# A sparse-attention block: one two-column addition for a coming tile's threshold and the present tile's sum

## The chip, the cores and the metric

The kernel runs on one core of a Trainium2 chip. What is measured is the device time of one execution in microseconds (us). The core has five engines that each work through their own queue in order: PE (TensorE, matrix products and transposes), DVE (VectorE), ACT (ScalarE), POOL (GpSimd) and SP (SyncE, which here only issues transfers). "PEld" is the loading of PE's weights, which runs beside PE.

## What is computed

The reference is an attention that keeps only scores near the largest of their row, then two feed-forward blocks, the second with a Fourier transform:

```python
scores = scale * np.matmul(q, k.transpose(0, 1, 3, 2))
thresh = np.max(scores, axis=-1, keepdims=True) - tau
scores = np.where(scores >= thresh, scores, -1000000000.0)
scores = scores - np.max(scores, axis=-1, keepdims=True)
attn = np.exp(scores)
attn = attn / (np.sum(attn, axis=-1, keepdims=True) + 1e-09)
return np.matmul(attn, v).astype(np.float32)
...
k = np.maximum(xk @ w_k, 0.0)
v = k * k @ w_v
r = 1.0 / (1.0 + np.exp(-(xr @ w_r)))
return (r * v).astype(np.float32)
...
X = np.fft.fft(np.fft.fft(x, axis=1), axis=2)
u = x + np.real(X)
```

with q, k and v of 4 batches, 8 heads, 576 rows and 64 columns, d_model 512, d_ff 1024, and a last feed-forward pair of 512 by 2048 weights after a normalization of u. Only the attention is touched by the change.

## The kernel before, in words

The heads go in 16 pairs (4 batches by 4 pairs). A pair has nine score tiles of 128 query rows by 576 keys, so there are 144 tiles, called steps n = 0 to 143. The fifth tile of a pair, "em", holds the 64 last rows of both heads.

For each tile, PE makes the scores into a PSUM tile "s" (lines 227 and 241). DVE takes the negated row maximum from it (line 267). A threshold, maximum minus tau, is made from that by one small instruction on DVE (line 274), or for one tile of nine on ACT (line 272, chosen by the bit mask `TH`). ACT writes exp(score - maximum) into an SBUF tile "e" (line 278). DVE multiplies e by the mask "score at least threshold" and accumulates the row sum at the same time (line 282, which also shows as a short DVE_READ_ACCUMULATOR). Then DVE adds 1e-9 to the sum (line 633) and takes the reciprocal (line 637), and POOL, or ACT for some tiles, multiplies e by it (lines 289, 290 and 643). Two steps later PE transposes e (lines 329, 337, 349 and 352), ACT copies the result to SBUF "pt" and "ptr", and PE multiplies it with v ("av", line 388). All three small columns of a tile lie in one SBUF tile, "small", in nine groups of three.

Tiles 0 to 35 (batch 0) use plain float32 matmuls, and while they run PE has nothing but attention; DVE also splits the weights w_k and w_r into two parts meanwhile (lines 69 to 71, "wbits"), with ACT and POOL behind it (lines 75 and 79). In this stretch three score tiles are in flight, and the maximum is taken two steps ahead (`LX` is 2); from about step 34 on it is one step ahead and two score tiles are in flight. From the second batch on, the first feed-forward block of the batch before ("kps", "rps", "vps", lines 408 to 410 and 530 to 532) runs between the attention steps on PE, fed by "xtmp" and "xl" (lines 437 to 441), and w_v is split. Each later head pair loads "rawqk" into a single buffer, which DVE's line 196 frees. After the last step the transform and the last feed-forward block follow.

The order of all instructions is set by a scheduler at build time: the program emits the steps in a loop, each part with a priority offset from the table `P`, and the scheduler plays them through its own model and lays down a fixed order for each engine. The table is the same in both kernels. On an engine, an instruction that waits holds back all that stand behind it.

The functions that matter are `emit_max`, `emit_th`, `emit_exp`, `emit_select` and `emit_norm`, and `do_front`, which calls them for each step.

Of the kernel before, what the change touches and what calls it, by code (L numbers as in the profile page):

```python
# [10 lines left out]
F32 = mybir.dt.float32  # L11
F32R = mybir.dt.float32r
I32 = mybir.dt.int32
ALU = mybir.AluOpType
# [15 lines left out]
def tile_kernel(ctx: ExitStack, tc: tile.TileContext, a):  # L30
# [11 lines left out]
    small = const.tile([128, 46], F32, name="small")  # L42
    mus, cons, stats = small[:, 0:16], small[:, 16:19], small[:, 19:46]
# [103 lines left out]
    heads, vts, ptu, ptr, et, em, sps, stat, xT = ({} for _ in range(9))  # L147
# [116 lines left out]
    def emit_max(n):  # L264
        st = stats[:, 3 * (n % 9):3 * (n % 9) + 3]
        stat[n] = st
        dve.tensor_reduce(st[:, 0:1], sps[n][:, :, 0:HS], axis=AX.XY, op=ALU.max, negate=True)  # L267

    def emit_th(n):
        st = stat[n]  # L270
        if P['TH'] >> (n % 9) & 1:
            act.activation(st[:, 1:2], st[:, 0:1], AF.Identity, scale=-1.0, bias=cons[:, 1:2])
        else:
            dve.tensor_scalar(st[:, 1:2], st[:, 0:1], -1.0, cons[:, 1:2], op0=ALU.mult, op1=ALU.add)

    def emit_exp(n):
        st = stat[n]
        act.activation(two(eview(n)), sps[n][:, :, 0:HS], AF.Exp, bias=st[:, 0:1])  # L278

    def emit_select(n):  # L280
        st, e = stat[n], two(eview(n))
        dve.scalar_tensor_tensor(  # L282
            e, sps[n][:, :, 0:HS], st[:, 1:2], e, op0=ALU.is_ge, op1=ALU.mult, accum_out=st[:, 2:3]
        )

    def emit_norm(n):
        st, e = stat[n], eview(n)
        if n in em:
            pool.tensor_scalar(em[n][:, S:640], e[:, 512:S], st[:, 2:3], 1.0, op0=ALU.mult, op1=ALU.mult)
        pool.tensor_scalar(e, e, st[:, 2:3], 1.0, op0=ALU.mult, op1=ALU.mult)  # L290

    def emit_front(n):

        cur, nxt = 0 <= n < NSTEP, 0 <= n + 1 < NSTEP
        if cur:
            emit_select(n)
        if nxt:
            emit_max(n + 1)
        if cur:
            dve.tensor_scalar(stat[n][:, 2:3], stat[n][:, 2:3], 1e-9, None, op0=ALU.add)  # L300
        if nxt:
            emit_th(n + 1)
        if cur:
            dve.reciprocal(stat[n][:, 3:4], stat[n][:, 2:3])
            emit_norm(n)
# [263 lines left out]
    act.dma_start(cons[:, 2:3], a["tau"].to_broadcast([128, 1]))  # L569
    load_head(0, 0)  # L570
    load_head(0, 1, act, act)
    dve.memset(stats[:, 26:27], 0.0)
    act.activation(stats[:, 26:27], stats[:, 26:27], AF.Exp)

    tau = cons[:, 2:3]
    dve.tensor_scalar(cons[:, 0:1], tau, 0.0, 0.125, op0=ALU.is_ge, op1=ALU.mult)
    dve.tensor_scalar(cons[:, 1:2], tau, -1.0, 0.0, op0=ALU.mult, op1=ALU.min)
# [24 lines left out]
    for n in range(P['LX']):  # L602
        emit_max(n)
        emit_th(n)
        emit_exp(n)
# [10 lines left out]
    def do_front(n, pi, s):  # L616
# [3 lines left out]
        k = 1  # L620
        if s != 4 and P['SM' if pi >= NPAIR else 'SM0'] >> ((s - (s > 4)) // 2) & 1:

            k = 0 if s in (0, 2, 5, 7) else 2
        g = stats.rearrange("p (s c) -> p s c", c=3)[:, s + 1 - k:s + 1]
# [3 lines left out]
        with hp('pM'):  # L628
            for m in nxt:
                emit_max(m)  # L630
        with hp('pF'):
            if cur and k:
                dve.tensor_scalar(g[:, :, 2], g[:, :, 2], 1e-9, None, op0=ALU.add)
            for m in nxt:
                emit_th(m)
            if cur and k:
                dve.reciprocal(g[:, :, 2], g[:, :, 2])  # L637
        with hp('pN'):
            for m in range(n + 1 - k, n + 1):
                if cur:  # L640
# [723 lines left out]
```

## Time and profile before

| | us |
|---|---|
| median of 3 runs (1053.62 to 1055.33) | 1053.88 |
| the profiled execution, its own time | 1055.04 |
| its span, first to last instruction | 1053.0 |
| PE busy in the span | 1003.0 (95%) |
| DVE busy | 717.3 (68%) |
| ACT busy | 536.3 (51%) |
| POOL busy | 395.4 (38%) |

The shares are averages over stages with different limits: attention of batch 0 until about 118 us, attention with the first feed-forward block until about 510 us, and the transform with the last feed-forward block after that. In a row of the profile "idle before" is the time in which the engine stood still just ahead of these instructions, and after the arrow stands what ended it. A duration in the timeline runs from an instruction's start to its end; the next one on the same engine may start before that end, since an engine overlaps instructions that don't wait for each other. "PEclk" is the share of TensorE's full clock that was granted: 1.00 is 2.4 GHz.

### The profile page before, as it was taken

What the parts mean: (1) busy time and instruction counts of PE and PEld (TensorE: products, weight loads), DVE (VectorE), ACT (ScalarE), POOL (GpSimd) and SP (SyncE); (2) the same over time, 40 slices, a digit from 0 to 9 for tenths busy, and PEclk for the clock granted to TensorE, in tenths of its full rate; (3) what the DMA queues carried; (4) which work ended last, traced back from release to release, by engine and by line L of the source; (5) the groups of instructions that cost most, each with busy time, mean ns of one, the idle gap of its engine ahead of it and who ended that gap; (6) DMA issues with size and microseconds to landing.
All of it is one profiled execution on the core that took longest, in us unless ns stands there. A gap on an engine that the chain in (4) does not pass through costs nothing.

```text
span 1053.0 us, 18827 instructions
## 1 busy us (share of the span) xinstructions
PE 1003.0 (95%) x6807; PEld 884.1 (84%) x6807; DVE 717.3 (68%) x1880; ACT 536.3 (51%) x1211; POOL 395.4 (38%) x495
## 2 busy tenths in 40 slices
PE   6887779999999999999999989999999999999998
PEld 4565659988889888999889879898998888889997
DVE  6799988667776685865356889457537449236776
ACT  4688777675866766857265745243313113113332
POOL 1445868465584564844233100000014125112231
PEclk9899989999999999999999989999999999999999
DMA  6442332121211212100613666536325335223221
GB/s 228 146 133 80 118 108 60 48 67 43 72 60 48 73 31 88 51 24 14 198 55 110 202 204 200 159 127 207 119 92 180 130 119 175 96 101 120 101 100 61
DMA packets 45636, 114.52 MB, mean 109 GB/s; under 512 B 6319, under 2 KB 6740, under 8 KB 45544
## 3 DMA queue, kind: packets, MB, share of 16 engines
q1 hardware_dynamic: 27920, 74.47, 22.2%
q10 hardware_dynamic: 12344, 22.13, 6.8%
q0 software_dynamic: 5280, 16.72, 4.4%
q8 instruction: 54, 0.88, 0.4%
q14 instruction: 38, 0.31, 0.1%
HBM read 84.98 MB, written 28.32 MB: 108 GB/s over the span
## 4 chain that ended last, share of the span: by engine, by line
PE 74%; DVE 10%; DMA 6%; ACT 3%; issue 3%; POOL 2%; SPq 0%; ACTq 0%; DVEq 0%; POOLq 0%
PE c1ps L1090 7%; PE c1ps L1089 6%; PE c1ps L1088 6%; PE s L227 5%; PE av L388 5%; PE c2ps L1112 5%; PE c2ps L1110 5%; PE c2ps L1111 5%; PE p L1045 4%; PE t L329 4%; PE kps L408 2%; PE kps L409 2%; PE kps L410 2%; DMA rawqk<-in_qk 2%; PE vps L530 2%
## 5 line engine op out<-in xcount | busy, mean ns | idle before, releaser
L267 DVE TENSOR_REDUCE small<-s 128x1 f32<-128x576 f32 x144 | 106.9, 752 | 48.1 <-PE s L227 37.3
L1159 POOL DMA_DIRECT2D ud<-u x54 | 29.5, 546 | 264.2 <-DVE u L1158 206.3
L290 POOL TENSOR_SCALAR e<-e,small 128x576 f32<-128x576 f32 x112 | 90.1, 811 | 87.9 <-DVE small L637 73.5
L282 DVE SCALAR_TENSOR_TENSOR e<-s,small,e 128x576 f32<-128x576 f32 x128 | 102.7, 812 | 25.6 <-ACT e L278 22.4
L278 ACT ACTIVATE e<-s,small 128x576 f32<-128x576 f32 x128 | 93.9, 745 | 31.1 <-DVE small L267 27.9
L1100 ACT ACTIVATE hh<-c1ps 128x256 fp32r<-128x256 f32 (+1 forms) x84 | 37.1, 443 | 137.2 <-PE c1ps L1090 111.6
L1101 DVE SCALAR_TENSOR_TENSOR hh<-c1ps,hh 128x256 fp32r<-128x256 f32 (+1 forms) x84 | 41.6, 496 | 89.2 <-ACT hh L1100 89.2
L329 PE MATMUL t<-ident,e 128*128 128x128 f32 x512 | 82.5, 278 | 12.9 <-ACT pt L332 6.5
L332 ACT ACTIVATE pt<-t 128x512 f32<-128x512 f32 x128 | 75.2, 599 | 22.3 <-PE t L329 20.6
L329 PEld LDWEIGHTS t<-ident,e 128*128 128x128 f32 x512 | 61.2, 142 | 24.3 <-issue 6.9
L488 POOL TENSOR_TENSOR k<-relu,k 128x288 fp32r<-128x288 f32 x64 | 54.3, 851 | 68.1 <-ACT k L486 63.9
L408 PE MATMUL kps<-xh,wk 128*128 128x288 f32 x256 | 78.1, 306 | 1.7 <-DVE tg L537 0.9
L530 PE MATMUL vps<-k,wv 128*128 128x288 f32 x256 | 77.5, 304 | 0.4 <-ACT tg L518 0.4
L531 PE MATMUL vps<-k,wv 128*128 128x288 f32 x256 | 77.3, 303 | 0.0
L532 PE MATMUL vps<-k,wv 128*128 128x288 f32 x256 | 76.7, 301 | 0.0
L410 PE MATMUL kps<-xh,wk 128*128 128x288 f32 x256 | 76.2, 298 | 0.0
L409 PE MATMUL kps<-xl,wk 128*128 128x288 f32 x256 | 76.2, 298 | 0.0
L1090 PE MATMUL c1ps<-ut,cB 128*128 128x256 f32 (+1 forms) x256 | 76.0, 297 | 0.0
L1089 PE MATMUL c1ps<-ut,cB 128*128 128x256 f32 (+1 forms) x256 | 75.8, 296 | 0.0
L1088 PE MATMUL c1ps<-ut,cB 128*128 128x256 f32 (+1 forms) x256 | 75.7, 296 | 0.0
L1088 PE MATMUL c1ps<-ut,cA 128*128 128x256 f32 (+1 forms) x224 | 71.0, 317 | 1.4 <-ACT ut L1008 1.4
L1089 PE MATMUL c1ps<-ut,cA 128*128 128x256 f32 (+1 forms) x224 | 70.7, 316 | 0.0
(270 smaller groups left out, 3116.4 us busy)
## 6 DMA issues: line engine op xcount, KB each, us to landing
u<-ud SPq DMA_DIRECT2D x36, 512.0 KB
wraw<-in_w_ch ACTq DMA_DIRECT2D x64, 256.0 KB
rawqk<-in_qk SPq DMA_DIRECT2D x24, 608.0 KB
ud<-u POOLq DMA_DIRECT2D x54, 256.0 KB, 2.5
v<-in_v SPq DMA_DIRECT2D x16, 320.0 KB
un<-ud SPq DMA_DIRECT2D x18, 256.0 KB
out<-u SPq DMA_DIRECT2D x18, 256.0 KB
wraw<-in_w_k SPq DMA_DIRECT2D x8, 512.0 KB
```

The costliest lines, as they stand in the source:

```text
L267: dve.tensor_reduce(st[:, 0:1], sps[n][:, :, 0:HS], axis=AX.XY, op=ALU.max, negate=True)
L278: act.activation(two(eview(n)), sps[n][:, :, 0:HS], AF.Exp, bias=st[:, 0:1])
L282: dve.scalar_tensor_tensor(e, sps[n][:, :, 0:HS], st[:, 1:2], e, op0=ALU.is_ge, op1=ALU.mult, accum_out=st[:, 2:3])
L290: pool.tensor_scalar(e, e, st[:, 2:3], 1.0, op0=ALU.mult, op1=ALU.mult)
L329: pe.transpose(t[:, k, :], e[:, o + 128 * k:o + 128 * (k + 1)], ident)
L408: pe.matmul(ps, wh, x[0][k], start=(k == 0), stop=False)
L409: pe.matmul(ps, wh, x[1][k], start=False, stop=False)
L410: pe.matmul(ps, wl, x[0][k], start=False, stop=(k == nk - 1))
L530: pe.matmul(ps, wv[0][:, c:c + 128], k2[0][:, k, :], start=(k == 0), stop=False)
L1088: pe.matmul(ps, wh, ut[0][:, k, :], start=(k == 0), stop=False)
L1089: pe.matmul(ps, wh, ut[1][:, k, :], start=False, stop=False)
L1090: pe.matmul(ps, wl, ut[0][:, k, :], start=False, stop=(k == 3))
```

## The change

The sign of the scores is turned: the factor applied to q is -0.125 instead of 0.125. The row maximum becomes a row minimum (without negation), which is at once the bias of exp, whose scale is now -1. The threshold becomes minimum plus max(tau, 0), and the mask "score at most threshold". With that, the threshold of a coming tile and the sum of the present tile both come from adding a constant to a column: the minimum of the coming tile and the sum of the present one are written side by side into a block of four columns, and one addition of two columns with the constants (max(tau, 0), 1e-9) makes the threshold and the sum plus 1e-9, again side by side. The separate threshold instruction on DVE (line 274) or ACT (line 272) and the separate addition (line 633) are gone; the reciprocal stays. At the very start two tiles get a one-column addition, and one memset of a column is added.

```diff
-    small = const.tile([128, 46], F32, name="small")
-    mus, cons, stats = small[:, 0:16], small[:, 16:19], small[:, 19:46]
+    small = const.tile([128, 56], F32, name="small")
+    mus, cons, stats = small[:, 0:16], small[:, 16:20], small[:, 20:56]
...
-    def emit_max(n):
-        st = stats[:, 3 * (n % 9):3 * (n % 9) + 3]
-        stat[n] = st
-        dve.tensor_reduce(st[:, 0:1], sps[n][:, :, 0:HS], axis=AX.XY, op=ALU.max, negate=True)
-
-    def emit_th(n):
-        st = stat[n]
-        if P['TH'] >> (n % 9) & 1:
-            act.activation(st[:, 1:2], st[:, 0:1], AF.Identity, scale=-1.0, bias=cons[:, 1:2])
-        else:
-            dve.tensor_scalar(st[:, 1:2], st[:, 0:1], -1.0, cons[:, 1:2], op0=ALU.mult, op1=ALU.add)
+    def block(n):
+        return stats[:, 4 * (n % 9):4 * (n % 9) + 4]
+
+    def emit_min(n, at_step):
+        low[n] = block(at_step)
+        dve.tensor_reduce(low[n][:, 0:1], sps[n][:, :, 0:HS], axis=AX.XY, op=ALU.min)
+
+    def emit_add(n, ahead, cur):
+        c0, c1 = 0 if ahead else 1, 2 if cur else 1
+        g = block(n)
+        dve.tensor_tensor(g[:, 2 + c0:2 + c1], g[:, c0:c1], cons[:, 1 + c0:1 + c1], op=ALU.add)
...
-        act.activation(two(eview(n)), sps[n][:, :, 0:HS], AF.Exp, bias=st[:, 0:1])
+        act.activation(two(eview(n)), sps[n][:, :, 0:HS], AF.Exp, scale=-1.0, bias=low[n][:, 0:1])
...
-            e, sps[n][:, :, 0:HS], st[:, 1:2], e, op0=ALU.is_ge, op1=ALU.mult, accum_out=st[:, 2:3]
+            e, sps[n][:, :, 0:HS], low[n][:, 2:3], e, op0=ALU.is_le, op1=ALU.mult, accum_out=block(n)[:, 1:2]
...
             for m in nxt:
-                emit_max(m)
+                emit_min(m, n)
         with hp('pF'):
-            if cur and k:
-                dve.tensor_scalar(g[:, :, 2], g[:, :, 2], 1e-9, None, op0=ALU.add)
-            for m in nxt:
-                emit_th(m)
-            if cur and k:
-                dve.reciprocal(g[:, :, 2], g[:, :, 2])
+            if cur or nxt:
+                emit_add(n, len(nxt), cur)
+            if cur:
+                r = block(n)[:, 3:4]
+                dve.reciprocal(r, r)
```

The scheduler lays the order anew. Line numbers differ between the two kernels: the reduction is line 267 before and 269 after, the mask 282 and 281, the reciprocal 637 and 616, a transpose 329 and 313, and the new addition is line 274. First DVE's queue at the fourth weight piece of the first stretch ("wbits" is the weight, "small" the columns). Before:

```order
L267 TENSOR_REDUCE small<-s 128x1
L274 TENSOR_SCALAR small<-small 128x1
L267 TENSOR_REDUCE small<-s 128x1
L282 SCALAR_TENSOR_TENSOR e,small<-s,small,e 128x576
L69 TENSOR_SCALAR wbits<-wraw 128x512
L633 TENSOR_SCALAR small<-small 128x1
L70 SCALAR_TENSOR_TENSOR wbits<-wraw,wbits 128x512
L637 RECIPROCAL small<-small 128x1
L282 SCALAR_TENSOR_TENSOR e_368,small<-s,small,e_368 128x576
```

The same place after:

```order
L269 TENSOR_REDUCE small<-s 128x1
L71 SCALAR_TENSOR_TENSOR wbits<-wraw,wbits 128x512
L274 TENSOR_TENSOR small<-small 128x2
L616 RECIPROCAL small<-small 128x1
L281 SCALAR_TENSOR_TENSOR e,small<-s,small,e 128x576
L69 TENSOR_SCALAR wbits<-wraw 128x512
L379 COPY xt<-xt 128x1
L70 SCALAR_TENSOR_TENSOR wbits<-wraw,wbits 128x512
```

Two small instructions have become one, and it stands behind the reduction of a later tile; the reciprocal stands straight behind the addition, whose result it reads. Next PE's queue at the start of the program ("s" scores, "t" transposes). Before:

```order
L227 MATMUL s<-k,q 128x288 x8
L329 MATMUL t<-ident,e 128x128 x4
L241 MATMUL s<-k,q 128x288 x3
L241 MATMUL s<-k,q 128x224
L241 MATMUL s<-k,q 128x64
L227 MATMUL s<-k,q 128x288 x4
```

After:

```order
L227 MATMUL s<-k,q 128x288 x8
L241 MATMUL s<-k,q 128x288 x3
L241 MATMUL s<-k,q 128x224
L241 MATMUL s<-k,q 128x64
L227 MATMUL s<-k,q 128x288 x2
L313 MATMUL t<-ident,e 128x128 x4
```

The first four transposes have moved behind the scores of two more tiles. Last DVE's queue in the middle of the attention with the feed-forward block. Before:

```order
L267 TENSOR_REDUCE small<-s 128x1 x2
L274 TENSOR_SCALAR small<-small 128x1
L282 SCALAR_TENSOR_TENSOR e,small<-s,small,e 128x576 x2
L633 TENSOR_SCALAR small<-small 128x1 x2
L637 RECIPROCAL small<-small 128x1 x2
L537 SCALAR_TENSOR_TENSOR tg<-tg,vps 128x288
```

After:

```order
L269 TENSOR_REDUCE small<-s 128x1 x2
L274 TENSOR_TENSOR small<-small 128x2
L616 RECIPROCAL small<-small 128x1
L281 SCALAR_TENSOR_TENSOR em,small<-s,small,em 128x576
L274 TENSOR_TENSOR small<-small 128x2
L616 RECIPROCAL small<-small 128x1
```

Before, two tiles went through side by side, mask and mask, addition and addition; after, each tile's addition and reciprocal follow one another, and the next tile's mask comes behind them.

## Rows read from the trace of the kernel before

**Rows 1.** Share of busy tenths in 40 slices of the span.

```profile
PE   6887779999999999999999989999999999999998
...
DVE  6799988667776685865356889457537449236776
```

**Rows 2.** Busy time by stretch: start:end, length, each engine's busy time (count), PEclk.

```profile
12.00:40.00 28.00, 21.39 (x97) 14.27 (x96) 23.02 (x71) 16.46 (x31) 12.39 (x14) 0.88 0.59 194
40.00:80.00 40.00, 35.84 (x212) 25.95 (x211) 38.50 (x110) 32.43 (x67) 17.61 (x19) 1.00 0.41 123
80.00:110.00 30.00, 24.20 (x152) 16.66 (x151) 27.96 (x81) 23.14 (x46) 16.83 (x19) 1.00 0.34 100
110.00:150.00 40.00, 31.61 (x221) 26.41 (x219) 36.21 (x84) 27.79 (x62) 32.71 (x35) 0.96 0.34 105
150.00:510.00 360.00, 354.58 (x2712) 318.57 (x2713) 251.46 (x691) 247.46 (x564) 204.14 (x259) 1.00 0.17 52
```

**Rows 3.** DVE's groups from 12 to 150 us: busy, mean ns, idle before.

```profile
L267 DVE TENSOR_REDUCE small<-s 128x1 f32<-128x576 f32 x46 | 34.2, 747 | 1.5 <-PE s L227 1.3
L282 DVE SCALAR_TENSOR_TENSOR e<-s,small,e 128x576 f32<-128x576 f32 x39 | 31.5, 809 | 1.7 <-ACT e L278 1.3 <-ACT small L272 0.2
...
L274 DVE TENSOR_SCALAR small<-small 128x1 f32<-128x1 f32 x39 | 8.0, 206 | 0.2
...
L633 DVE TENSOR_SCALAR small<-small 128x1 f32<-128x1 f32 x45 | 6.4, 143 | 0.1
```

**Rows 4.** DVE's timeline at 17 us: start, duration; the next starts before the end.

```profile
17.17 0.21 DVE L274 TENSOR_SCALAR small<-small 128x1 f32<-128x1 f32 x1
17.29 0.14 DVE L633 TENSOR_SCALAR small<-small 128x1 f32<-128x1 f32 x1
17.35 0.68 DVE L71 SCALAR_TENSOR_TENSOR wbits<-wraw,wbits 128x512 int32<-128x512 int32 x1
```

**Rows 5.** DVE's timeline at 49 us: the reciprocal reads the addition ahead of it.

```profile
49.21 0.15 DVE L633 TENSOR_SCALAR small<-small 128x1 f32<-128x1 f32 x1
49.39 0.16 DVE L637 RECIPROCAL small<-small 128x1 f32<-128x1 f32 x1
```

**Rows 6.** DVE's timeline at 581 us, an addition of two columns in a later stage.

```profile
580.83 0.16 DVE L990 TENSOR_TENSOR lnst<-lnst 128x2 f32<-128x2 f32 x1
580.90 0.45 DVE L810 TENSOR_TENSOR H<-f,H 128x288 fp32r<-128x288 f32 x1
```

**Rows 7.** The chain that ended last, 10 to 150 us: shares by line, one piece.

```profile
by line: issue 9.6%; DVE e L282 8.2%; DVE small L267 8.1%; DMA wraw<-in_w_v 8.0%; PE s L227 7.9%; PE avs L388 6.9%; DMA rawqk<-in_qk 6.4%; PE t L329 3.9%; DVE wbits L71 3.7%; DVE wbits L69 3.5%; ACT e L278 3.4%; DVE wbits L70 3.3%; PE s L24
...
81.23 4.95 DMA rawqk<-in_qk
```

**Rows 8.** PE's timeline, 28 to 37 us.

```profile
30.00 1.11 PE L349 MATMUL tm<-ident,em 128*128 128x128 f32 x4 [3.27 <-POOL em L290]
...
33.92 3.53 PE L388 MATMUL avs<-pt,v 128*64 128x288 f32 x16
```

**Rows 9.** PE's timeline, 80 to 83 us: the same sixteen matmuls.

```profile
80.98 2.11 PE L388 MATMUL avs<-pt,v 128*64 128x288 f32 x16
```

**Rows 10.** Groups from 150 to 510 us: DVE's reduction, PE's transposes, POOL's multiplication.

```profile
L267 DVE TENSOR_REDUCE small<-s 128x1 f32<-128x576 f32 x98 | 72.8, 754 | 46.3 <-PE s L227 35.7 <-PE s L241 10.0
...
L329 PE MATMUL t<-ident,e 128*128 128x128 f32 x352 | 57.2, 274 | 0.2 <-ACT pt L356 0.2
...
L290 POOL TENSOR_SCALAR e<-e,small 128x576 f32<-128x576 f32 x88 | 69.6, 799 | 75.4 <-DVE small L637 61.1 <-DVE small L633 14.2
```

**Rows 11.** PE's timeline at 282 us: the spacing of feed-forward matmuls.

```profile
282.16 0.30 PE L409 MATMUL kps<-xl,wk 128*128 128x288 f32 x1
...
283.09 0.29 PE L410 MATMUL kps<-xh,wk 128*128 128x288 f32 x1
```

**Rows 12.** SP's queue around 100 us: issues of transfers.

```profile
98.55 0.33 SPq L56 DMA_DIRECT2D wraw<-in_w_v  x1
103.78 0.33 SPq L163 DMA_DIRECT2D rawqk<-in_qk  x1
```

More of the change, by code (lines that the diff above doesn't have):

```diff
@@ L146, in tile_kernel @@
     NSTEP = NPI * 9
-    heads, vts, ptu, ptr, et, em, sps, stat, xT = ({} for _ in range(9))
+    heads, vts, ptu, ptr, et, em, sps, low, xT = ({} for _ in range(9))
     def plain(pi):
@@ L276, in emit_exp @@
+    def emit_min(n, at_step):
[5 more added lines that the diff above has]
+        dve.tensor_tensor(g[:, 2 + c0:2 + c1], g[:, c0:c1], cons[:, 1 + c0:1 + c1], op=ALU.add)
     def emit_exp(n):
-        st = stat[n]
-        act.activation(two(eview(n)), sps[n][:, :, 0:HS], AF.Exp, bias=st[:, 0:1])
+        act.activation(two(eview(n)), sps[n][:, :, 0:HS], AF.Exp, scale=-1.0, bias=low[n][:, 0:1])
@@ L280, in emit_select @@
     def emit_select(n):
-        st, e = stat[n], two(eview(n))
+        e = two(eview(n))
         dve.scalar_tensor_tensor(
-            e, sps[n][:, :, 0:HS], st[:, 1:2], e, op0=ALU.is_ge, op1=ALU.mult, accum_out=st[:, 2:3]
+            e, sps[n][:, :, 0:HS], low[n][:, 2:3], e, op0=ALU.is_le, op1=ALU.mult, accum_out=block(n)[:, 1:2]
         )
     def emit_norm(n):
-        st, e = stat[n], eview(n)
+        r, e = block(n)[:, 3:4], eview(n)
         if n in em:
-            pool.tensor_scalar(em[n][:, S:640], e[:, 512:S], st[:, 2:3], 1.0, op0=ALU.mult, op1=ALU.mult)
@@ L290, in emit_norm @@
[L290 to L305, printed above, removed]
+            pool.tensor_scalar(em[n][:, S:640], e[:, 512:S], r, 1.0, op0=ALU.mult, op1=ALU.mult)
@@ L307, in unit @@
+        pool.tensor_scalar(e, e, r, 1.0, op0=ALU.mult, op1=ALU.mult)
     def unit(pi, half):
@@ L566, in ffn_stream @@
         yield from xt_out()
-    act.dma_start(cons[:, 2:3], a["tau"].to_broadcast([128, 1]))
+    act.dma_start(cons[:, 3:4], a["tau"].to_broadcast([128, 1]))
     load_head(0, 0)
     load_head(0, 1, act, act)
[L572 to L577, printed above, removed]
+    dve.memset(stats[:, 35:36], 0.0)
+    act.activation(stats[:, 35:36], stats[:, 35:36], AF.Exp)
+    dve.memset(cons[:, 2:3], 1e-9)
+    tau = cons[:, 3:4]
+    dve.tensor_scalar(cons[:, 0:1], tau, 0.0, -0.125, op0=ALU.is_ge, op1=ALU.mult)
+    dve.tensor_scalar(cons[:, 1:2], tau, 1.0, 0.0, op0=ALU.mult, op1=ALU.max)
     conv_k(0, 0)
@@ L602, in tile_kernel @@
     for n in range(P['LX']):
-        emit_max(n)
-        emit_th(n)
+        emit_min(n, n - P['LX'])
+        emit_add(n - P['LX'], True, False)
         emit_exp(n)
@@ L619, in do_front @@
         state['m'] = max(state['m'], n + ahead(n) + 1)
[L620 to L624, printed above, removed]
         with hp('pF'):
@@ L629, in do_front @@
             for m in nxt:
-                emit_max(m)
+                emit_min(m, n)
         with hp('pF'):
-            if cur and k:
-                dve.tensor_scalar(g[:, :, 2], g[:, :, 2], 1e-9, None, op0=ALU.add)
-            for m in nxt:
-                emit_th(m)
-            if cur and k:
-                dve.reciprocal(g[:, :, 2], g[:, :, 2])
-        with hp('pN'):
-            for m in range(n + 1 - k, n + 1):
-                if cur:
-                    if P['NA' if pi >= NPAIR else 'NA0'] >> (m % 9) & 1:
-                        e = eview(m)
-                        act.activation(e, e, AF.Copy, scale=stat[m][:, 2:3])
-                    else:
-                        emit_norm(m)
+            if cur or nxt:
[3 more added lines that the diff above has]
+                dve.reciprocal(r, r)
+        with hp('pN'):
+            if cur:
+                if P['NA' if pi >= NPAIR else 'NA0'] >> (n % 9) & 1:
+                    e = eview(n)
+                    act.activation(e, e, AF.Copy, scale=r)
+                else:
+                    emit_norm(n)
     def do_av(n, pi, s):
```

## The prediction, made before the changed kernel was run

> **What bounds the kernel now.** I read the busy shares by slice first. PE stands at nine tenths or more from the seventh slice on (a slice is 26.3 us) with two exceptions, and only the first six slices, up to about 158 us, lie below; there DVE has 9, 9 and 9 in the third to fifth [rows 1]. The table of stretches gives the sizes: from 12 to 150 us PE is busy 21.39 + 35.84 + 24.20 + 31.61 = 113.0 of 138 us, DVE 23.02 + 38.50 + 27.96 + 36.21 = 125.7, which is 91% [rows 2]. From 150 to 510 us PE is busy 354.6 of 360 us, so that 5.4 us is all that any other engine could give back there [rows 2]. After 510 us no instruction of the change runs. So the change is judged by the stretch from 12 to 150 us, in which PE idles 25 us.
>
> The chain of waits warns against taking DVE's 91% as the whole truth. In its shares for 10 to 150 us the named DVE lines (mask 8.2%, reduction 8.1%, weight split 3.7, 3.5 and 3.3%) with "issue" 9.6% make 36%; the rest are transfers of w_v and rawqk, PE and ACT, such as a rawqk transfer of 4.95 us that began at 81.23 [rows 7]. "Issue" pieces I count to DVE, since they lie between DVE's pieces. DVE's time therefore counts on the path with a weight between 0.36 and 0.91.
>
> **What the change takes away and adds.** *On DVE, per tile.* The threshold instruction lasts 206 ns, the addition of 1e-9 143 ns [rows 3]. But what they hold DVE for is less: the threshold starts at 17.17, the next instruction at 17.29, and the one behind the addition at 17.35, so the slots are 0.12 and 0.06 us [rows 4]. The new addition of two columns has a near relative in a later stage: 0.16 us long, the next instruction 0.07 us after its start [rows 6]. From 12 to 150 us 39 thresholds and 45 additions go, and about 46 new additions come, one for each reduction [rows 3]. Slots: 39 x 0.12 + 45 x 0.06 - 46 x 0.07 = 4.68 + 2.70 - 3.22 = 4.2 us less on DVE.
>
> *The hold.* An instruction that reads the result of the one straight ahead of it waits for its end: the reciprocal at 49.39 stands 0.18 us behind the addition at 49.21, not 0.07 [rows 5]. So a held place costs 0.11 us. In the laid-down order of the first 46 tiles 10 of the small instructions wait for the one straight ahead before, and 20 after (12 reciprocals, 8 additions). The 10 more cost 1.1 us. Net 4.2 - 1.1 = 3.1 us.
>
> Bounds of the new instruction: if none of the new ones were held longer than now, 4.2 us are gained. If every new addition held its follower (46 x 0.18 instead of 46 x 0.07), it would be 4.68 + 2.70 - 8.28 = -0.9 us, that is 0.9 us lost. I take 3.1 us, because the order says how many are held, and the 0.07 us row is the same operation on the same number of columns.
>
> *On the path.* 3.1 us x 0.36 = 1.1 us to 3.1 x 0.91 = 2.8 us. I take 2.8, since DVE's queue is what stands full from 40 to 110 us (66.5 of 70 us busy [rows 2]).
>
> *On ACT.* One tile in nine had its threshold made by ACT; the mask waited 0.2 us for that in this stretch [rows 3]. The wait goes: 0.2 us. Sum: 2.8 + 0.2 = 3.0 us.
>
> *At nothing.* The turned sign: reduction, exp, mask and the factor on q are the same instructions on as many elements with other constants. The memset of one column lies in the wait for the first inputs. From 150 to 510 us DVE loses about as much by slots as it gains by holds (99 tiles less, 151 held places against 82 by the order), and PE's 354.6 of 360 us covers the rest; without that cover up to 2 us would show.
>
> *Moved queues.* On SP's queue the third rawqk transfer (issued at 103.78, after a w_v piece at 98.55 [rows 12]) now stands behind one more w_v piece, and the fifth behind all eight. A w_v piece waits there until DVE has split the one before it, so a rawqk behind it starts some 4 us later. It is loaded a head pair ahead, and nine steps take 9 x 360 / 98 = 33 us in the long stretch [rows 2, 10], so I cost it at nothing; if that cover failed it would be 4 us once or twice. On POOL's queue the multiplication of the first "em" tile moves one 0.75 us multiplication ahead. PE's first four transposes move behind two tiles' scores; nothing on PE uses them before the first product with v.
>
> *The added wait.* The present tile's sum now goes through an instruction that also needs the coming tile's minimum, hence its scores on PE. Behind it wait the reciprocal, POOL's multiplication, and two steps later PE's transposes. From 150 to 510 us the reduction waits for scores 46.3 us in all, 0.47 us on each of 98 tiles, while transposes waited 0.2 us in all [rows 10]. What covers it is PE's own order: between the scores of a tile and the transposes of the one before it there stand at least 18 other PE instructions, before and after the change alike, typically some 50. At 0.133 us each (the first and the eighth of a series start at 282.16 and 283.09, 0.93 / 7 [rows 11]) 18 give 2.4 us. The way through is reduction 0.75, addition and reciprocal 0.2 each, POOL 0.75 to 0.8, about 2.0 us with no second tile ahead on POOL. It fits, barely at the worst five places. So no cost, but this is where a loss would come from.
>
> **A rule against my slots.** Rows 4 show the next independent instruction starting well before the end of a small one, rows 5 that a wait costs 0.11 us. The Trainium skill, VectorE: DVE Perf Modes, section "The DRAIN you can't avoid", says that the next operation does not start before the pipeline has emptied and that a semaphore after each of eight copies cost nothing extra; by it full durations count and holds are free. The same section allows that an operation that is not held starts earlier. The trace disagrees with the first half where nothing waits (0.12 us against 206 ns). What full durations would make of it, from rows: 39 x 0.206 + 45 x 0.143 - 46 x 0.157 = 8.03 + 6.44 - 7.22 = 7.2 us, x 0.91 = 6.6 us. I hold that as the first rival.
>
> **The sum.** Against the profiled execution's own time: 1055.0 - 3.0 = 1052.0 us. That execution lies 1.16 us above the median of the runs, 1053.88, so for a median 1053.88 - 3.0 = 1050.9 us.
>
> **The rivals.**
> - *Full durations count* (or one of PE's early gaps closes with it): 1053.88 - 6.6 - 0.2 = 1047.1 us. For it: DVE at 91%, and early in the program em's multiplication comes sooner. Against: rows 4. Chance 0.12.
> - *The path is transfers and PE, and DVE's time is not on it*, or the holds eat the slots: between 0.9 lost and 1.1 gained, so 1053.9 us. For it: the chain's 36%. Chance 0.18.
> - *Slower by an early gap on PE with the clock behind it.* Normalizing a tile now needs the scores of the tile two steps ahead, and in the first stretch PE is short of work. Before, PE waited 3.27 us for POOL ahead of the transposes at 30.00, and afterwards 16 matmuls took 3.53 us [rows 8] that take 2.11 us at full clock [rows 9]; the granted clock of 12 to 40 us was 0.88 [rows 2], a mix of 2.4 and 1.2 GHz. One more such gap costs 3.27 + 1.42 for these matmuls, and about 1.7 more for the score and transposes around them, estimated at the same ratio: 6.4 us. 1053.9 - 3.0 + 6.4 = 1057.3 us. It decides once POOL's end lies later than PE's work ahead of the transposes. Against: PE's order has more scores ahead of the first transposes now. Chance 0.18.
> - *Slower in the long stretch.* If a sixth of the 46.3 us for which the reduction waits came through to the transposes, 7.7 us: 1053.9 - 3.0 + 7.7 = 1058.6 us. It decides at the places with only 18 instructions of cover. For it: POOL's multiplication already waits 75.4 us for DVE [rows 10]. Against: transposes waited 0.2 us. Chance 0.12.
> - That the change doesn't do what it says I give no chance of its own: the order shows one addition for each tile and no threshold on ACT.
>
> **How the numbers follow.** The forecast, 0.40: 1050.9 us, its own range 1049.5 (4.2 + 0.2 gained) to 1052.6 (1.1 + 0.2). A measurement of this kernel can tell about 0.2%, 2.1 us, from no change: below 1051.8 is faster, above 1056.0 slower. Of the forecast three quarters lie below 1051.8: 0.30 faster, 0.10 same. With the first rival faster is 0.42, with the second same is 0.28, and the two slower ones make 0.30. The range for 8 in 10 runs from 1046.5, just beyond the first rival, to 1058, between the two slower ones.
>
> **What would show it.** Right: on DVE about 146 additions of two columns with slots near 0.07 us where the next is independent and 0.18 us where the reciprocal follows; the busy time of DVE down by 10 to 15 us over the span (128 x 0.12 + 144 x 0.06 - 146 x 0.07 = 13.8) but the time by 3 us; the first feed-forward product on PE some 3 us earlier than now; no ACT instruction for a threshold. Wrong: transposes waiting for POOL by more than 2 us from 150 to 510 us, a granted clock below 0.88 from 12 to 40 us, or PE's idle time from 12 to 150 us not below 25 us.

## The result, and the profile after

The changed kernel takes 1067.19 us (median of 5 runs, 1064.73 to 1067.97), the kernel before 1054.64 us beside it. The ratio is 1.0116, with a 95% interval of 1.0101 to 1.0131: 12.2 us slower, where the prediction had 3.0 us faster and a range that ended at 1058.0. The profiled execution has a span of 1065.4 us against 1053.0. Ratios are of executions within 1.5% of the fastest of their kernel; the one trace of run e9 is of an execution of 1241 us, and is not read.

The busy time by stretch, after (start:end, length, busy time and count of PE, PE's weight loads, DVE, ACT, POOL, then the granted clock of PE):

```profile
12.00:40.00 28.00, 21.95 (x102) 14.46 (x101) 23.92 (x64) 17.07 (x33) 9.14 (x12) 0.88 0.52 178
40.00:80.00 40.00, 35.27 (x187) 24.25 (x187) 35.13 (x84) 26.40 (x51) 18.41 (x19) 0.91 0.42 125
80.00:110.00 30.00, 24.42 (x125) 16.66 (x126) 26.01 (x66) 21.61 (x42) 14.65 (x17) 0.90 0.27 78
110.00:150.00 40.00, 30.67 (x180) 23.27 (x179) 36.50 (x80) 27.20 (x59) 28.64 (x33) 0.82 0.37 107
150.00:510.00 360.00, 352.83 (x2711) 318.46 (x2712) 260.37 (x614) 250.41 (x561) 211.02 (x262) 1.00 0.18 55
```

Against [rows 2] PE's busy time hardly moves (112.3 us from 12 to 150 us, 113.0 before), and whoever reads that alone sees nothing. The counts do move. A matmul that runs across a border counts in both of its stretches, so the four stretches are taken as one, first before, then after:

```profile
12.00:150.00 138.00, 113.03 (x677) 83.29 (x676) 125.69 (x343) 99.82 (x203) 79.55 (x86) 0.96 0.41 127
12.00:150.00 138.00, 112.31 (x593) 78.64 (x592) 121.56 (x291) 92.27 (x182) 70.85 (x80) 0.88 0.39 120
```

PE is as busy with 84 matmuls less. At 0.133 us each (an estimate, from the spacing in [rows 11]) that is 11.2 us, about the whole loss, and it is lost before the long stretch, where the count is as before (2711, 2712). PE idles no longer than before either: 138 - 112.3 = 25.7 us against 25.0. What changed is how fast its matmuls ran: the clock of the last three stretches fell from 1.00, 1.00 and 0.96 to 0.91, 0.90 and 0.82. With two levels, 2.4 and 1.2 GHz, these shares put PE at the lower one for some 34 of the 138 us, against 10 before.

The tiles tell the same. The start of the reduction of a tile, after less before, in us:

| tile | 12 | 18 | 21 | 27 | 33 | 36 | 39 | 48 | 143 |
|---|---|---|---|---|---|---|---|---|---|
| changed kernel | -0.6 | -0.2 | +4.0 | +6.1 | +8.3 | +10.4 | +13.8 | +9.7 | +9.3 |

DVE's groups from 12 to 150 us, after, which answer to [rows 3]:

```profile
L269 DVE TENSOR_REDUCE small<-s 128x1 f32<-128x576 f32 x43 | 32.1, 750 | 4.6 <-PE s L227 3.3 <-PE s L241 1.1
...
L274 DVE TENSOR_TENSOR small<-small 128x2 f32<-128x2 f32 (+1 forms) x43 | 13.2, 308 | 0.3
```

The new addition should have lasted 0.16 us [rows 6]. It lasts 0.308 us on average. Two places show why. DVE and POOL at 59 us, in order of start (start, duration, engine, line):

```profile
59.20 1.27 POOL L79 TENSOR_TENSOR wk<-wbits,wk 128x512 fp32r<-128x512 f32 x1
59.32 0.08 DVE L281 DVE_READ_ACCUMULATOR e<-s,small,e 128x1 f32 x1
59.32 1.17 DVE L274 TENSOR_TENSOR small<-small 128x2 f32<-128x2 f32 x1
...
60.52 0.16 DVE L616 RECIPROCAL small<-small 128x1 f32<-128x1 f32 x1
...
71.02 1.27 POOL L79 TENSOR_TENSOR wr<-wbits,wr 128x512 fp32r<-128x512 f32 x1
...
71.57 0.74 DVE L274 TENSOR_TENSOR small<-small 128x2 f32<-128x2 f32 x1
72.34 0.16 DVE L616 RECIPROCAL small<-small 128x1 f32<-128x1 f32 x1
```

POOL's instruction ends at 60.47, the addition at 60.49; at 72.29 and 72.31 the second time. The addition began while POOL computed, and ended when POOL did. In the whole span 63 additions begin so, 38 of them last over 250 ns, up to 1297 ns; of the other 25, 17 began with less than 0.21 us of POOL's instruction left. Of the old thresholds and additions, half of which also began with POOL at work, none lasted over 223 ns. The Trainium skill, SBUF — State Buffer, section "Who interferes with whom", has this as a rule: a DVE instruction with two inputs in SBUF contends with a POOL instruction that reads SBUF, for ports that the two share and that whoever comes first holds alone. The trace agrees to 0.02 us for the 38. The other eight began with 452 to 765 ns of POOL's instruction (line 421 or 182) left and took 146 to 155 ns all the same; in six of them POOL's own instruction was the longer one, 0.60 to 1.10 us where most others of its line take 0.51 and 0.81.

The trace of before showed it as well, in lines that I passed over. The weight split's two instructions there, 12 to 150 us:

```profile
L70 DVE SCALAR_TENSOR_TENSOR wbits<-wraw,wbits 128x512 int32<-128x512 int32 x19 | 15.9, 836 | 0.1
L71 DVE SCALAR_TENSOR_TENSOR wbits<-wraw,wbits 128x512 int32<-128x512 int32 x18 | 15.2, 842 | 0.1
```

They read two tensors in SBUF. One of them takes 0.68 us at 17.35 [rows 4], the group's mean is 842 ns, and the longest 1725 ns. The 17 during which POOL stood idle took 674 to 694 ns; the 20 others took 969 ns on average.

The second thing to see is the coupling. Tile 17's mask (L281) starts at 58.59; its reciprocal (L616) is the one at 67.11. The timeline of the changed kernel:

```profile
58.59 0.79 DVE L281 SCALAR_TENSOR_TENSOR e<-s,small,e 128x576 f32<-128x576 f32 x1
...
65.89 0.76 DVE L269 TENSOR_REDUCE small<-s 128x1 f32<-128x576 f32 x1 [0.56 <-PE s L227]
66.68 0.16 DVE L274 TENSOR_TENSOR small<-small 128x2 f32<-128x2 f32 x1
67.11 0.16 DVE L616 RECIPROCAL small<-small 128x1 f32<-128x1 f32 x1
67.36 0.75 POOL L289 TENSOR_SCALAR e<-e,small 128x576 f32<-128x576 f32 x1 [1.81 <-DVE small L616]
68.16 0.42 PEld L313 LDWEIGHTS t<-ident,e 128*128 128x128 f32 x4 [0.59 <-POOL e L289]
68.17 0.66 PE L313 MATMUL t<-ident,e 128*128 128x128 f32 x4 [0.36 <-POOL e L289]
```

The mask was done at 59.4, but addition and reciprocal stand behind the reduction of tile 19, which waits for scores until 65.89; POOL and PE's transposes wait behind them. Before, the mask was done at 59.8 and the reciprocal came at 61.1. Worked out from the starts and ends of every tile, the time from the mask's end to the reciprocal is 2.1 us for tiles 0 to 17 and 2.0 us for 18 to 35 before, 4.6 and 4.9 us after. And PE's scores wait longer for the masks that free their banks. PE's waits for DVE of 12 to 150 us, after (what waited, for whom, us, times, longest):

```profile
PE s L227 <- DVE e L281: 7.6, 7, 1.9
...
PE s L227 <- DVE small L616: 2.7, 1, 2.7
...
PE s L241 <- DVE e L281: 2.3, 2, 1.8
...
PE s L227 <- DVE em L281: 1.0, 2, 0.8
```

The same before:

```profile
PE s L227 <- DVE e L282: 3.8, 5, 1.7
...
PE s L227 <- DVE em L282: 0.9, 1, 0.9
...
PE s L241 <- DVE e L282: 0.2, 1, 0.2
```

That is 13.6 us in which scores wait for DVE, against 4.9 before. The transposes wait that much less, 10.9 us in all against 18.1, which is why PE's idle time stays. The sixteen matmuls that take 2.11 us in [rows 9] show what the lower clock does:

```profile
118.01 3.70 PE L372 MATMUL avs<-pt,v 128*64 128x288 f32 x16
```

They lie in a stretch whose granted clock of 0.82 is a mix of 2.4 and 1.2 GHz. With 24 us more at the lower level, PE busy for 0.81 of the time and 1 - 2.11 / 3.70 of that lost, the clock makes some 8 of the 12 us (an estimate). From 40 to 150 us it falls six times, each time shortly behind a gap of over 1 us on PE, such as the 2.71 us in which a score waits for DVE until 82.51. But in the kernel before, gaps of 1.58 us until 88.06 and 2.39 us until 106.23 brought no fall. So it isn't shown which gap costs the clock, and the clock is told here as the form that the loss takes on PE, not as its cause.

### The profile page after: what moved, and what is told of

The parts are those of the page before. It is cut to its first block, busy times and chain, and to the rows that moved or that the text cites. A ratio compares the mean times of both kernels' runs of the same rounds, so it can differ in the third digit from the quotient of the medians.

```text
span 1065.4 us, 18602 instructions
## 1 busy us (share of the span) xinstructions
PE 1011.8 (95%) x6807; PEld 889.8 (84%) x6807; DVE 724.5 (68%) x1755; ACT 535.5 (50%) x1195; POOL 396.1 (37%) x495
## 4 chain that ended last, share of the span: by engine, by line
PE 69%; DVE 13%; DMA 9%; POOL 3%; issue 3%; ACT 2%; SPq 0%; DVEq 0%; ACTq 0%; POOLq 0%
PE av L372 6%; PE c1ps L1066 6%; PE c1ps L1068 6%; PE c1ps L1067 6%; PE s L227 5%; PE c2ps L1089 4%; PE c2ps L1088 4%; PE c2ps L1090 4%; PE p L1023 4%; PE t L313 4%; PE kps L392 2%; DMA wraw<-in_w_ch 2%; PE kps L394 2%; PE kps L393 2%; DMA rawqk<-in_qk 2%
## 5 line engine op out<-in xcount | busy, mean ns | idle before, releaser
L281 DVE SCALAR_TENSOR_TENSOR e<-s,small,e 128x576 f32<-128x576 f32 x128 | 103.1, 806 | 21.8 <-ACT e L277 18.7
```

The source lines that it names most:

```text
L281: dve.scalar_tensor_tensor(e, sps[n][:, :, 0:HS], low[n][:, 2:3], e, op0=ALU.is_le, op1=ALU.mult, accum_out=block(n)[:, 1:2])
```

## The experiments

Ratios are to the kernel before on the same chip, with 95% intervals; 0.001 is 1.05 us.

**Is it the coupling? Two separate additions.** After this edit the reciprocal no longer waits (from mask to reciprocal 2.3 and 1.9 us). Two more runs do it for some of the tiles, one (e2) for those below 36, the other (e3) for those from 36 on, and one (e4) joins the sum to a threshold that is ready:

```
-    emit_add(n, len(nxt), cur)
+    emit_add(n, False, True)     # sum + 1e-9
+    emit_add(n, True, False)     # threshold
```

> The changed kernel, but the threshold of the coming tile and the sum of the present one are added by two separate one-column additions, so that the sum and the reciprocal no longer wait for the coming tile's minimum; sign, blocks and the missing ACT threshold stay as changed. Theory A (the coupling: a tile's normalization waits for the scores two tiles ahead, and PE's transposes and later scores wait for the normalization): about 1054 to 1056 us, PE's granted clock from 40 to 150 us back near 1.00 and 0.96. Theory B (the turned sign, the blocks of four or the missing ACT threshold re-lay the order on the engines unfavourably): 1064 to 1068 us as the changed kernel.

> Two separate additions for tiles below 36 (the stretch before the feed-forward work), the joined addition behind that. Theory A, with the loss made before 150 us: 1053 to 1056 us. Rival C (the loss comes from the coupling in the long stretch, tiles 36 to 143): 1063 us or more.

> The reverse: the joined addition for tiles below 36, two separate additions from tile 36 on. Theory A: still 1061 to 1067 us (the masks of tiles 19 to 35 come some 4 to 9 us later than before, and what tiles 36 to 40 add to that may go). Rival C: about 1054 us.

> The joined addition stays, but it joins the present tile's sum to the threshold of the next tile, not of the second next: in the early stretch that minimum was reduced one step before, so that nothing new is waited for; from tile 36 on it is as in the changed kernel. Theory A: 1051 to 1055 us (no wait, and the slots on DVE saved). Theory B: 1064 to 1068 us.

Measured: 1.0120 (1.0090 to 1.0151), 1.0077 (1.0056 to 1.0099), 1.0073 (1.0048 to 1.0098) and 1.0129 (1.0109 to 1.0149). Theory A, the coupling as the whole loss, falls: without it the kernel is as slow. But the tiles moved. With separate additions tile 27 is 0.4 us early instead of 6.1 late, and the loss comes later (+4.1 at tile 36, +11.4 at 39). The additions' row from 12 to 150 us of that run sent me to POOL:

```profile
L274 DVE TENSOR_TENSOR small<-small 128x1 f32<-128x1 f32 x86 | 23.5, 281 | 0.1
```

Twice as many additions, each stretched as before: 86 x (0.281 - 0.150) = 11 us of DVE's time, against 43 x (0.308 - 0.157) = 6.5 us in the changed kernel. This run had exchanged one cost for the other.

**Is it the second tensor?** First the two separate additions in a form that reads one tensor, then the same with the coupling put back, then the kernel before with nothing but the form of its addition changed, and with nothing but the sign:

```
e5  + dve.tensor_scalar(block(n)[:, 3:4], block(n)[:, 1:2], 1e-9, None, op0=ALU.add)
    + dve.tensor_scalar(block(n)[:, 2:3], block(n)[:, 0:1], 1.0, cons[:, 1:2], op0=ALU.mult, op1=ALU.add)
e6  + dve.tensor_scalar(block(n)[:, 3:4], block(n)[:, 1:2], 1e-9, block(n)[:, 0:1], op0=ALU.add, op1=ALU.max)
e7  - dve.tensor_scalar(g[:, :, 2], g[:, :, 2], 1e-9, None, op0=ALU.add)
    + dve.tensor_tensor(g[:, :, 2], g[:, :, 2], cons[:, 3:4], op=ALU.add)
```

> As the run with two separate additions, but both in a form that reads one tensor (tensor with a scalar) instead of two. In the trace of the changed kernel 38 of the 60 additions that begin while POOL computes last over 250 ns (up to 1297 ns) and end some 17 ns after POOL's instruction; in the kernel before none of the 128 thresholds lasts over 223 ns and none of the 144 additions over 158 ns. Theory P (an addition of two tensors in SBUF on DVE waits for the end of POOL's running instruction): no small addition over 250 ns, 1053 to 1057 us. Rival O (the loss is that the instructions are laid in another order on the engines, as it is here too): 1062 to 1068 us.

> As the run with two one-input additions, but the addition of 1e-9 also takes the maximum with the coming tile's minimum (which is negative, while the sum is at least 1, so the value stays), so that the sum and the reciprocal wait for the coming scores as in the changed kernel. It shows the coupling without the second tensor. By the masks of tiles 21 to 33, which came 4 to 8 us later in the changed kernel and 0 to 4 us later with two separate additions: 3 to 7 us above the run without the coupling, 1057 to 1062 us. If the coupling costs nothing: as that run.

> The kernel before with one edit: the addition of 1e-9 reads a second tensor (a column that holds 1e-9) in place of a constant. The order of the instructions on every engine stays the same as in the kernel before, but for one memset at the start. Theory P: 40 to 50 of the 144 additions stretched to 0.4 to 1.3 us, some 20 us more DVE time in all, and 1059 to 1066 us. Rival O (the order): 1053.6 us.

> The kernel before with the turned sign alone (minimum in place of the negated maximum, exp with scale -1, mask with less-or-equal); the order on every engine stays the same. All theories: 1053.6 us, within 2 us.

Measured: 1.0006 (0.9997 to 1.0015), 1.0068 (1.0051 to 1.0085), 1.0044 (1.0028 to 1.0059), 0.9992 (0.9980 to 1.0003). The turned sign costs nothing. The third run is the clean one, since every engine has its instructions in the order of before. Its addition from 12 to 150 us, the same 45 as in [rows 3], 143 ns there:

```profile
L634 DVE TENSOR_TENSOR small<-small 128x1 f32<-128x1 f32 x45 | 13.1, 292 | 0.1
```

45 x (0.292 - 0.143) = 6.7 us more on DVE, and 4.6 us (2.9 to 6.2) more time. So the second tensor costs by itself, and DVE's time counted with 4.6 / 6.7, about 0.7. In the traces only 3.3 us of it are there at tile 48, near 155 us, so up to that place the weight is nearer to 0.5. I had expected 1059 to 1066 us and got 1059.4, the low end; 37 additions lasted over 250 ns, where I expected 40 to 50.

**A control that failed, and a version that is faster.** The control for the coupled run has its instructions without its wait (the maximum is taken with the tile's own minimum). Two runs leave the addition of 1e-9 out (which changes no value, since the sum holds exp(0) = 1, and 1 + 1e-9 is 1 in float32), the second of them with all thresholds on DVE, and one makes the threshold later:

```
e9      max with low[n][:, 0:1] in place of block(n)[:, 0:1]
e10, 11 - dve.tensor_scalar(g[:, :, 2], g[:, :, 2], 1e-9, None, op0=ALU.add)
e11     also 'TH': 0 in place of 'TH': 4 in the table P: no threshold on ACT
e12     e5 with emit_min(m, m - 1): the threshold of n + 1 at step n
```

> Control for the coupled one-input run: the same instructions, but the maximum is taken with the present tile's own minimum, which has long been there, so that nothing new is waited for. If the 6.5 us that the coupled run lies above the uncoupled one are the coupling: 1054 to 1057 us. If they are the longer slot of an addition that reads a column as its scalar (0.12 instead of 0.06 us for some 45 tiles before 150 us, 2.7 us): 1057 to 1059 us. Where the order of the instructions, which is another one again, were the cause: 1059 us or more.

> The kernel before without the addition of 1e-9 (the sum holds the term exp(0) = 1, and 1 + 1e-9 is 1 in float32). One DVE instruction per tile less, no second tensor, no coupling: what the change was to save, without either wait. By the slots of 0.06 us, 45 x 0.06 = 2.7 us before 150 us, of which 0.7 count by the run with two inputs (6.3 us of stretching there, 4.4 us of time): 1.9 us, so 1052 to 1054 us beside a run of the kernel before at 1054 to 1055. If the slots hide behind PE and transfers: no difference.

> As the run without the addition, and the threshold that ACT made for one tile in nine is made on DVE too. Five more slots of 0.12 us before 150 us (0.6 us) against waits of 0.2 us for ACT: within 1 us of that run, unless the order, which is laid anew, counts: then it differs by more than 2 us.

> As the run with two one-input additions, but the threshold of the next tile is made one step later than there, behind the present tile's sum, as in the run in which the joined addition took the threshold whose minimum was ready (1066.6 us, which the wait for POOL alone, about 5 us, doesn't explain). Theory L (a threshold made only between two masks lengthens the chain from mask to mask): 1058 to 1062 us. Rival: 1054 to 1057 us, and that run's remaining loss has another cause.

Measured: 1.0062 (1.0044 to 1.0081), 0.9968 (0.9956 to 0.9980), 1.0014 (1.0003 to 1.0024), 1.0013 (1.0001 to 1.0025). The control without any coupling is as slow as the coupled run, so that run proves nothing of the coupling. Two kernels that differ by the engine of one threshold in nine (e10, e11) lie 5 us apart (1050.57 and 1055.64). I had expected less than 1, or more than 2 if the order counts. The order in which the instructions are laid moves with such an edit, and I put the difference down to it; no run takes the order by itself. Leaving the addition out is the one version that beats both kernels, 3.4 us (2.1 to 4.6) under the kernel before. A threshold made late costs about nothing in this run (e12).

**How much is the second tensor in the changed kernel itself?** The joined addition gets a constant in place of the second tensor, with the order of the changed kernel (the threshold then leaves out tau, so these kernels compute other values with the same instructions); the same for the two separate additions; then the coupling for some of the tiles, and the ready threshold:

```
e13, e14  - dve.tensor_tensor(g[:, 2 + c0:2 + c1], g[:, c0:c1], cons[:, 1 + c0:1 + c1], op=ALU.add)
          + dve.tensor_scalar(g[:, 2 + c0:2 + c1], g[:, c0:c1], 1e-9, None, op0=ALU.add)
e15, e16  that joined addition for tiles below 36 (e15) or from 36 on (e16), e5's two for the others
e17       that addition in e4
```

> The changed kernel with one edit: the joined addition of two columns adds the constant 1e-9 to both in place of a second tensor (the threshold leaves out tau). The order of the instructions is that of the changed kernel on every engine, and the coupling stays. Theory P says what the wait for POOL costs there: by the 6.5 us of stretching before 150 us, about 4 to 6 us, so 1061 to 1063 us. What is left over the kernel before (1054 to 1055 us) is then the coupling and the order that it brings: 6 to 8 us. If the wait for POOL were all: 1054 to 1056 us.

> The run with two separate additions of two tensors (1065.2 us), both turned into an addition of a constant (the threshold leaves out tau); the order stays that of that run on every engine. Theory P: 1054 to 1057 us, since nothing is coupled. Rival O (part of that run's loss was its order): 1058 us or more.

> No second tensor; the joined addition (of the constant, the threshold leaves out tau) for tiles below 36 alone, two one-input additions behind. Theory K (the reciprocal behind the coming minimum: from the mask's end to the reciprocal 4.8 us instead of 2.0 for tiles 0 to 35 in the changed kernel): most of the coupling's cost, so 1058 to 1062 us. If the early coupling is hidden: 1054 to 1056 us.

> The reverse: two one-input additions for tiles below 36, the joined addition of the constant from tile 36 on. Theory K, with PE's long queue covering the wait there (reciprocal 2.0 us behind the mask instead of 0.8): 1054 to 1057 us. Rival C (the long stretch pays too): 1058 us or more.

> One joined addition per tile of the constant 1e-9 (no second tensor, the threshold leaves out tau), joined with the threshold whose minimum is ready: neither the wait for POOL nor the wait for the coming scores, but the same number of instructions as in the changed kernel. Theory K (what is left beside the wait for POOL is the late reciprocal before tile 36): 1054 to 1057 us, tile 36 reduced within 3 us of the kernel before. Rival J (joining itself, or the order laid anew, costs): 1061 us or more, as the run with the ready minimum and two tensors (1066.6 us).

Measured: 1.0114 (1.0094 to 1.0134), 1.0049 (1.0031 to 1.0068), 1.0080 (1.0060 to 1.0100), 1.0145 (1.0124 to 1.0166), 1.0148 (1.0123 to 1.0174). Only e15 came within the range of its main theory. e13 and e14 came between or beyond the outcomes that I had named, e16 and e17 went to the rivals that I had named for them. The additions' rows from 12 to 150 us say why. First the changed kernel with a constant, then the two separate additions with a constant:

```profile
L274 DVE TENSOR_SCALAR small<-small 128x2 f32<-128x2 f32 (+1 forms) x43 | 13.2, 309 | 0.3
```

```profile
L274 DVE TENSOR_SCALAR small<-small 128x1 f32<-128x1 f32 x89 | 12.2, 144 | 0.2
```

An addition of a constant to two columns is stretched as much as one of two tensors (309 and 308 ns); to one column it is not (144 ns). So the joined runs e13 and e15 to e17 still had the wait for POOL, and can't speak of the coupling. Only e14 took it away: at the order of e1 the ratio fell from 1.0120 to 1.0049, 7.5 us, for the 11 us of stretching that went (again 0.7, though in the traces only 3.1 us of it are there at tile 48). The Trainium skill, VectorE: DVE Perf Modes, section "Mode 2×_2P — use both read ports for one tensor", says that a one-input instruction from SBUF to SBUF can use the second port when its outermost dimension of more than one element is even, or odd and the same at both ends. The two columns, stretched in these rows, agree with it; a single column has no such dimension.

**The joined addition without the wait.** Each value is laid beside its constant, and one reduction adds both pairs:

```
- dve.tensor_tensor(g[:, 2 + c0:2 + c1], g[:, c0:c1], cons[:, 1 + c0:1 + c1], op=ALU.add)
+ dve.tensor_reduce(g[:, 4 + c0:4 + c1], two(g[:, 0:4])[:, c0:c1], axis=AX.X, op=ALU.add)
```

> The changed kernel, with the joined addition written as a reduction: each of the two values lies beside its constant (threshold and sum in blocks of six columns), and one reduction adds both pairs; the output is complete. It reads one tensor and is a reduction, of which none is stretched in any run so far. The coupling stays, and the order on the engines is that of the changed kernel but for one copy at the start, one tile's addition early on DVE and two places early on PE and ACT. Theory P (the wait for POOL is the whole loss): no addition over 250 ns, 1053 to 1057 us. Theory K (the coupling and the order that comes with it cost 6 to 8 us beside the wait): 1060 to 1064 us. If the reductions of two columns are stretched behind POOL as well: 1065 to 1068 us, and the trace shows it.

Measured: 1060.05 us, 1.0068 (1.0054 to 1.0082). Its addition and its stretches from 12 to 150 us:

```profile
L274 DVE TENSOR_REDUCE small<-small 128x2 f32<-128x4 f32 (+1 forms) x45 | 6.7, 149 | 0.3
```

```profile
12.00:40.00 28.00, 21.12 (x109) 14.74 (x110) 26.00 (x72) 18.53 (x35) 11.56 (x13) 1.00 0.57 193
40.00:80.00 40.00, 33.67 (x189) 23.37 (x188) 34.18 (x90) 28.87 (x56) 19.50 (x20) 0.94 0.38 120
80.00:110.00 30.00, 25.04 (x131) 16.42 (x129) 24.56 (x63) 21.70 (x44) 13.57 (x16) 0.91 0.34 102
110.00:150.00 40.00, 31.51 (x195) 23.75 (x196) 33.79 (x79) 26.13 (x58) 31.23 (x34) 0.87 0.35 109
```

None of its 146 additions lasts over 161 ns, and the order is nearly that of the changed kernel. It is 1.0116 - 1.0068, 5.1 us, faster than the changed kernel (give or take 2.2, from the two intervals), which fits the 4.6 us of the clean run. That these 5.1 us are the wait for POOL is argued from that fit; the two traces don't show it place by place. The lead over the changed kernel grows from 0.7 us at tile 8 (24.6 us in the changed kernel) to 5.0 at tile 16 (53.5 us), where only some 1.0 us of stretching lies and the clock of 12 to 40 us is 1.00 against 0.88. From tile 18 to tile 48 (58 to 164 us) it goes from 5.1 to 5.6 us, while the changed kernel's additions are stretched by 6.6 us there. One place shows how a stretched addition can cost almost nothing. In the changed kernel:

```profile
26.97 0.63 DVE L274 TENSOR_TENSOR small<-small 128x2 f32<-128x2 f32 x1
27.61 0.54 DVE L69 TENSOR_SCALAR wbits<-wraw 128x512 int32<-128x512 int32 x1
```

With the reduction:

```profile
26.29 0.15 DVE L274 TENSOR_REDUCE small<-small 128x2 f32<-128x4 f32 x1
26.80 0.54 DVE L69 TENSOR_SCALAR wbits<-wraw 128x512 int32<-128x512 int32 x1 [0.36 <-POOL wk L79]
```

The addition is short, but the weight split behind it waits for the same instruction of POOL, and starts 0.81 us earlier than in the changed kernel, about the lead that this run had at tile 8.

The other 7.2 us (5.7 to 8.6) stay without any stretched addition. The rows show where: up to 40 us this kernel is ahead of the kernel before (109 matmuls against 97, tile 18 is reduced 5.2 us earlier), and it loses all from there on, 9.5 us late at tile 39, with PE's clock at 0.94, 0.91 and 0.87. Its reciprocals come 4.1 and 4.7 us behind the masks, as the changed kernel's.

What stays open is how those 7 us divide between the late reciprocal and the order that comes with it. By their times, runs with neither the stretching nor the coupling lie at 1.0006, 1.0013, 1.0049 and 1.0062 with four different orders; both runs that are coupled and not stretched lie at 1.0068. That is compatible with a coupling that costs 7 us and with one that costs less. The traces say a little more. At the start of tile 36's reduction the two that are coupled and not stretched (e6, e18) are 5.3 and 5.1 us later than the kernel before; the six that are neither in those tiles (e5, e10, e11, e12, e14, e16) lie between 1.0 us earlier and 2.5 us later; the three that are stretched and not coupled (e1, e2, e7) are 2.3 to 4.8 us late, the changed kernel 10.4. So by tile 36 the coupling goes with a loss of its own, of some 3 to 6 us, in one trace of each. Against it stands the control e9, as slow without a coupling. On one in-order queue the coupling is itself an order (the sum behind the coming minimum), and no run could have the one without moving the other.

Two more things are not settled. Joining to the ready threshold (e4, e17) is the slowest of all at tile 36, 14.5 and 15.0 us late, without any wait for coming scores; there the stretched addition stands between one tile's mask and the next one's. With an unstretched addition of its own at that place (e12) the threshold leaves tile 36 only 1.6 us late, but e12 joins nothing, so that the two can't be told apart. And joining only from tile 36 on (e16, 1.0145) is slower than joining everywhere (1.0114 with the same addition); that run's matmuls of 110 to 150 us fall to 157 at a clock of 0.74.

## Why the prediction was wrong, step by step

- *Slots and bounds of the new instruction: wrong, and the failed step that the runs show best.* The step "the 0.07 us row is the same operation on the same number of columns" took a row at which POOL stood idle. The bounds, 0.9 us lost to 4.2 gained, moved the holds and left the instruction's own length alone. It measured 0.308 us on average before 150 us, for 43 of them 6.5 us more than at the 0.157 us of the row that I used. The same edit in the kernel before (e7) prices such a stretching at 4.6 us of time; that the changed kernel pays about as much is argued from the run with the reduction.
- *The added wait at no cost: wrong in its reasoning.* I counted PE instructions between a tile's scores and the transposes of the one before, and found 2.4 us of cover for a 2.0 us way. That way runs over DVE's queue, which holds masks, weight pieces and factors on q in order. Measured, the reciprocal moved from 2.0 to 4.9 us behind its mask. What that costs by itself is inside the 7 us that stay, and how much of them it is stays open.
- *Fewer instructions: right in kind.* Without the addition of 1e-9 the whole kernel gains 3.4 us. In the run with the reduction tile 18 is 5.2 us earlier, though part of that is the clock (1.00 against 0.88 from 12 to 40 us). The weight for DVE's time, which I took as 0.91, measured 0.3 to 0.7, by the run and by where one reads it. DVE's busy time over the span, forecast to fall by 10 to 15 us, rose from 717.3 to 724.5 us with 125 instructions less: it held the waits.
- *The turned sign at nothing: right* (alone 0.9992). ACT's 0.2 us is too small to be told apart.
- *Moved queues and order at nothing: wrong.* An edit of one instruction per nine tiles (e10 to e11) moved the time by 5 us, mostly, as I argue, through the order. I had gone through the three or four moves that I could name and priced each at nothing; the others I had not priced at all.
- *The rivals.* The slower ones had the right sign and too small a size, 3.4 and 4.7 us of the 12.2. The kind of the first, a lower clock behind gaps on PE, is nearest to what the rows show, but from 40 us on and not before: the granted clock of 12 to 40 us is 0.88 as before. Of the second almost nothing came: from 150 to 510 us transposes waited 1.5 us for POOL's multiplication, 2.3 with a wait that ended at line 472, about the 2 us that I had set. Of the three signs for "wrong" the third came clearly, though only as PE's idle time staying: it is 25.7 us from 12 to 150 us, not below 25.

## What to carry to other kernels

Before counting an instruction at its shortest row, look whether it reads two tensors in SBUF on DVE, or adds a constant to two columns there, and how often POOL is at work meanwhile: the mean of a group of that kind against its shortest, as 842 against 680 ns here, tells it in the trace of before. Two short chains that are joined to save an instruction become one barrier on an in-order engine; leaving out what changes no bit (1 + 1e-9) saved a slot without a wait. And where a program lays the order anew for each edit, a forecast of a few us needs a range as wide as that order's own scatter, some 5 us here.

## What the runs showed of the hardware that was not expected

- Whether a small DVE instruction waits for POOL's end depends on its form: two tensors, 38 of the 63 that began while POOL computed stretched, up to 1297 ns; a constant on two columns, 309 ns on average before 150 us; a constant on one column, 144 ns; a column as scalar on one column, at most 228 ns; a reduction of 2 x 2 columns, at most 161 ns.
- A stretched addition ends 4 to 21 ns behind POOL's instruction, and DVE's queue stands until then: one of 0.16 us can hold it for 1.2 us. Where the next instruction waits for the same POOL instruction anyway, as at 27.61, that costs almost nothing.
